# Expert weights in 32 requests of 512 KB, two of them at the beginning, and a reordered start, in an attention and soft-MoE kernel

## The chip, the cores and the metric

The kernel runs on one core of a Trainium2 chip. The metric is the device time of one execution in microseconds (us), as the median of several executions. Beside it there is one execution under the profiler, with a row for each instruction and DMA packet; its times count from the start of its span.

## The reference: what is computed

Attention with 16 extra "beacon" keys and values in front of each head's own, then a soft mixture of experts on its output. Sizes: 8 batches, 8 heads, 576 tokens, head width 64, 16 beacons; 8 experts of 4 slots, width 512, hidden width 1024. All inputs are float32.

```python
k_all = np.concatenate([beacon_k, k], axis=2)      # [8, 8, 592, 64]
v_all = np.concatenate([beacon_v, v], axis=2)
scores = scale * np.matmul(q, k_all.transpose(0, 1, 3, 2))
scores = np.where(causal, -1000000000.0, scores)   # beacons are always seen
a = np.exp(scores - scores.max(-1, keepdims=True))
a /= a.sum(-1, keepdims=True) + 1e-09
attn = np.matmul(a, v_all)                          # -> x [4608, 512]
logits = x @ phi                                    # [4608, 32]
d = softmax over the 4608 tokens;  slot_input = d.T @ x
slot_out[e] = np.maximum(slot_input[e] @ w1[e], 0.0) @ w2[e]
c = softmax over the 32 slots;     out = c @ slot_out      # [4608, 512]
```

The weights w1 [8, 512, 1024] and w2 [8, 1024, 512] are 33.5 MB in float32; q, k and v are 28.3 MB, the output 9.4 MB.

## The kernel before, in words

The work goes by pairs of heads: 4 pairs a batch, 32 pairs in all, numbered n = 4b + g. The order of the instructions on each engine is the order of the calls in the source (a manual schedule), so a waiting instruction holds up everything behind it on its engine. Waits come from the tiles: a tile is free for its next writer when its last reader is done.

For a pair, `scores(n, bank)` (L469) runs the score products of one of four banks on PE, an exponential on ACT (L480) that writes `expT`, and a causal mask on POOL (`affine_select`, L488). `attend(n, hh)` (L493) multiplies by v, the "order products" of the change's name (L502); `normalize(n)` (L506) divides on DVE. `transposes(m, which)` (L445) turns a staged k or q (for two pairs, m = n // 2) on PE, copies it out on DVE (L465), and for k has POOL put two small blocks of beacon keys in front (L455). `cast_v(b, c)` (L378) casts a batch's v to fp16 on POOL in three steps (L384 twice, L388 for the remaining 80 tokens, tile `vrem`), and `perm_v(b)` (L390) reorders it with products on PE. Iteration n of the main loop (L641) holds the scores of pair n, the order products of pair n - 1, and, some pairs later, the transposes of x, `logits`, `dispatch` and `combine_T` of the mixture of experts.

Inputs come by requests of SP, in the order of the calls: `load_qk` (L343; k then q, 576 KB each for half a batch; for the very first half each is cut in two), `load_v` (L352; v, 1 MB, and `vrem`, 160 KB), `load_bv` (L374; beacon_v, 32 KB, into four partitions of the v tile, so that it waits for v to land). They are asked for two batches ahead, as tiles come free (k and q four tiles each, v two). SP's and ACT's requests share eight semaphores in turn, so a request also waits for the landing of the eighth before it. `bkf` (the beacon keys) and `phif` are asked for by ACT.

The weights are cast to fp16 as they are loaded, by requests of POOL: `load_weights(count)` (L430) takes the next `count` of the list `wchunks` (L408), 64 pieces of 256 KB (fp16). Five experts have tiles of their own; the last three go into the tiles of the last batches' k, q and v when those are free (`weight`, L414). Pair n asks for 2 if g = 0, else 1, and from n = 24 on for 2 or 3; what is left is asked for behind the loop (L689). POOL's requests too use eight semaphores in turn.

Behind the loop come the last transposes, logits and dispatch, the experts' first products (`first`, L715), the row sums for the last softmax (`row_sums`, L581, 9 products each), `turn`, the second products (`second`, L732, into `rsps`), and the output: 36 products with the scaling on ACT and DVE, 9.4 MB written by SP. `fill(count, by)` (L573) issues products whose result nobody reads; they stand where PE would have nothing to do.

## Time and profile before

| | us |
|---|---|
| median of 3 runs | 216.74 (215.91 to 219.17) |
| the profiled execution | 219.05 |
| its span, first to last instruction | 217.3 |
| PE busy | 167.5 (77%) |
| DVE, ACT, POOL busy | 134.4, 131.8, 129.4 |
| mean granted clock of PE | 0.90 |
| first order products (L502) | at 25.75 |
| last order products end | at 160.9 |
| second expert products (L736) | 174.2 to 186.3 |
| first product of the output (L797) | at 187.5 |

The profile page has busy time by engine, the span in 40 slices, the DMA queues, the chain of work that ended last, and the costliest groups of instructions. A group's row gives the engine, the operation, the tile written and the tiles read, how often, the busy time, and the idle time before it with what ended that. The slices before, busy tenths of PE, the granted clock, the DMA engines' share and what they moved:

```profile
PE   6932888889899899897897989989878972895400
PEclk9996599999999999999997999999999996587555
DMA  6999999999999999999999975799999999099992
GB/s 177 286 260 323 359 299 316 312 280 300 317 286 283 344 267 280 328 277 280 307 281 274 288 149 93 129 149 178 161 179 175 199 210 189 29 403 412 410 403 98
```

A slice is 5.4 us. GB/s counts what was written: a weight byte in fp16 stands for two read.

### The profile page before, as it was taken

What the parts mean: (1) busy time and instruction counts of PE and PEld (TensorE: products, weight loads), DVE (VectorE), ACT (ScalarE), POOL (GpSimd) and SP (SyncE); (2) the same over time, 40 slices, a digit from 0 to 9 for tenths busy, and PEclk for the clock granted to TensorE, in tenths of its full rate; (3) what the DMA queues carried; (4) which work ended last, traced back from release to release, by engine and by line L of the source; (5) the groups of instructions that cost most, each with busy time, mean ns of one, the idle gap of its engine ahead of it and who ended that gap; (6) DMA issues with size and microseconds to landing.
All of it is one profiled execution on the core that took longest, in us unless ns stands there. A gap on an engine that the chain in (4) does not pass through costs nothing.

```text
span 217.3 us, 7306 instructions
## 1 busy us (share of the span) xinstructions
PE 167.5 (77%) x3080; PEld 109.2 (50%) x3080; DVE 134.4 (62%) x274; ACT 131.8 (61%) x168; POOL 129.4 (60%) x291
## 2 busy tenths in 40 slices
PE   6932888889899899897897989989878972895400
PEld 1511454666666567466584756756755630241100
DVE  0452567787887888885895688888364110498500
ACT  2032587988897899787885889978911310394300
POOL 6027359788688579579576667997885310670000
PEclk9996599999999999999997999999999996587555
DMA  6999999999999999999999975799999999099992
GB/s 177 286 260 323 359 299 316 312 280 300 317 286 283 344 267 280 328 277 280 307 281 274 288 149 93 129 149 178 161 179 175 199 210 189 29 403 412 410 403 98
DMA packets 34309, 55.90 MB, mean 257 GB/s; under 512 B 7740, under 2 KB 16156, under 8 KB 34268
## 3 DMA queue, kind: packets, MB, share of 16 engines
q1 hardware_dynamic: 24444, 38.24, 53.6%
q0 software_dynamic: 9216, 16.78, 43.4%
q8 instruction: 26, 0.43, 0.7%
q10 hardware_dynamic: 608, 0.33, 0.6%
q14 instruction: 15, 0.12, 0.2%
HBM read 62.69 MB, written 9.44 MB: 332 GB/s over the span
## 4 chain that ended last, share of the span: by engine, by line
PE 53%; DMA 23%; ACT 8%; POOL 4%; issue 3%; DVE 2%; ACTq 0%; SPq 0%; POOLq 0%; DVEq 0%
PE av L502 14%; PE sc L475 13%; DMA wt<-in_moe_w_dram 10%; PE trps L463 8%; DMA vstag<-in_v_dram 6%; PE fps L797 5%; PE xtps L527 5%; DMA vstag<-in_beacon_v_dram 4%; ACT expT L480 4%; ACT vh L401 3%; DMA phif<-in_moe_phi_dram 3%; PE vpt L398 2%; PE sips L552 2%; PE lgps L539 2%; PE vps L398 1%
## 5 line engine op out<-in xcount | busy, mean ns | idle before, releaser
L480 ACT ACTIVATE expT<-sc 128x992 f16<-128x992 f32 (+3 forms) x128 | 104.4, 867 | 29.0 <-PE sc L475 27.9
L488 POOL TENSOR_SCALAR_AFFINE_SELECT expT<-expT 128x224 f16<-128x224 f16 (+3 forms) x128 | 55.2, 444 | 40.9 <-ACT expT L480 40.1
L475 PE MATMUL sc<-qT,kT 64*128 64x80 bf16 (+4 forms) x576 | 43.5, 248 | 11.6 <-ACT expT L480 6.0
L502 PE MATMUL av<-vh,expT 128*128 128x65 f16 (+1 forms) x960 | 41.9, 196 | 3.6 <-DVE x L516 1.6
L502 PEld LDWEIGHTS <-expT 128*128 128x128 f16 (+1 forms) x960 | 34.6, 99 | 7.8 <-POOL expT L488 2.7
L475 PEld LDWEIGHTS <-kT 64*128 64x128 bf16 x576 | 17.0, 95 | 27.9 <-issue 22.5
L465 DVE COPY qT<-trps 128x640 bf16<-128x640 bf16 (+1 forms) x32 | 23.3, 770 | 11.3 <-PE trps L463 11.3
L465 DVE COPY kT<-trps 128x640 bf16<-128x640 bf16 (+1 forms) x32 | 23.3, 771 | 10.3 <-PE trps L463 10.3
L516 DVE TENSOR_TENSOR x<-av,r 128x640 f16<-128x640 f32 x32 | 26.4, 825 | 1.2
L800 ACT ACTIVATE osb<-fps,rc 128x512 f32<-128x512 f32 x18 | 11.5, 690 | 17.1 <-PE fps L797 16.8
L384 POOL CAST vc<-vstag 128x512 f16<-128x512 f32 x32 | 18.7, 614 | 1.4 <-DMA vstag<-in_beacon_v_dram 1.4
L531 DVE COPY xT<-xtps 128x576 f16<-128x576 f16 x32 | 14.6, 458 | 6.9 <-PE xtps L527 6.9
L463 PE MATMUL trps<-idb,kstag 128*64 128x128 bf16 x288 | 12.3, 233 | 3.2 <-DMA kstag<-in_k_dram 3.1
L803 DVE TENSOR_SCALAR osb<-fps,rc 128x512 f32<-128x512 f32 x18 | 12.8, 747 | 2.3 <-PE fps L797 1.8
L527 PE MATMUL xtps<-idh,x 128*128 128x128 f16 (+2 forms) x160 | 13.8, 218 | 0.0
L797 PE MATMUL fps<-so,eT 128*128 128x512 f16 x36 | 12.9, 508 | 1.0 <-DVE so L757 0.8
L404 DVE CAST vh<-vpt 128x512 f16<-128x512 f32 x16 | 10.3, 685 | 5.4 <-PE vpt L398 5.4
L398 PE MATMUL vps<-vc,sel 32*128 32x512 f16 x64 | 10.2, 409 | 4.1 <-POOL vc L384 4.1
L401 ACT ACTIVATE vh<-vps 128x1024 f16<-128x1024 f32 x8 | 8.2, 1027 | 7.5 <-PE vpt L398 7.5
L463 PEld LDWEIGHTS <-kstag 128*64 128x64 bf16 x288 | 9.4, 117 | 6.4 <-DMA kstag<-in_k_dram 3.3
L463 PE MATMUL trps<-idb,qstag 128*64 128x128 bf16 x288 | 12.2, 232 | 0.0
L398 PE MATMUL vpt<-vc,sel 32*128 32x512 f16 x64 | 11.4, 407 | 0.3 <-issue 0.3
(87 smaller groups left out, 199.6 us busy)
## 6 DMA issues: line engine op xcount, KB each, us to landing
kstag<-in_k_dram SPq DMA_DIRECT2D x15, 576.0 KB, 14.3
qstag<-in_q_dram SPq DMA_DIRECT2D x15, 576.0 KB, 13.8
out_dram<-osb SPq DMA_DIRECT2D x11, 768.0 KB, 6.7
vstag<-in_v_dram SPq DMA_DIRECT2D x7, 1024.0 KB, 12.2
w1h<-in_moe_w_dram POOLq DMA_DIRECT2D x20, 256.0 KB, 7.3
w2h<-in_moe_w_dram POOLq DMA_DIRECT2D x20, 256.0 KB, 7.1
wt<-in_moe_w_dram POOLq DMA_DIRECT2D x16, 256.0 KB, 8.6
wv<-in_moe_w_dram POOLq DMA_DIRECT2D x8, 256.0 KB, 7.8
```

What stands on the lines that cost most here:

```text
L384: nc.gpsimd.tensor_copy(out=st["c", b][:, :, hs, :].rearrange("p t h d -> p h t d"), in_=st["v", b][:, hs, :, :])
L398: nc.tensor.matmul(outs[c], sel[32 * c:32 * c + 32, t, :], vc[32 * c:32 * c + 32, t, :, :].rearrange("p h d -> p (h d)"), start=(t == 0), ...
L401: nc.scalar.activation(vhs[b % 2][:, 0:2, :, 0:D], ps[:, :, :].rearrange("p c (h d) -> p c h d", d=D), AF.Copy)
L463: nc.tensor.transpose(tp[64 * hh:64 * hh + 64, j - j0, :], t[:, hh, j, :].bitcast(BF)[:, 1::2], idb[:, :])
L465: nc.vector.tensor_copy(out=dst.rearrange("p u (s j) -> p u s j", j=NJ)[:, :, :, j0:j1], in_=tp[:, :, :].rearrange("p j (u s) -> p u s j", ...
L475: nc.tensor.matmul(sc[:, hh, col:col + qw], kTs[n // 2 % 2][po:po + D, n % 2, c * P:(c + 1) * P], qTs[n // 2][po:po + D, n % 2, q0:q0 + qw ...
L480: nc.scalar.activation(ex[:, :, base:base + w], sc[:, :, 0:w], AF.Exp, scale=scale)
L488: nc.gpsimd.affine_select(out=ap, in_=ap, compare_op=AL.is_ge, fill=0.0, base=cbase, pattern=pat, channel_multiplier=-1)
L502: nc.tensor.matmul(av[:, i, :], exps[n % 2][0:KW[c], hh, o:o + P], vhs[b % 2][0:KW[c], c, h, :], start=(c == 0), stop=(c == i))
L516: nc.vector.tensor_tensor(out=xs[b][:, :, head(g, 0):head(g, 1) + 1:2, :].rearrange("p i h d -> p h i d"), in0=av[:, :, :, 0:D], in1=r[:, ...
L527: nc.tensor.transpose(tp[:, QLO[i]:QLO[i] + QW[i]], xs[b][0:QW[i], i, 2 * t:2 * t + 2, :].rearrange("p h d -> p (h d)"), idh[0:QW[i], 0:QW ...
L797: nc.tensor.matmul(fp_[:, :], row_tokens(bb, j), so1[:, :], start=True, stop=True)
```

## The change

1. Weights: 32 requests of 512 KB instead of 64 of 256 KB. A piece of w1 has two rows of 2 KB (fp16) per partition, a piece of w2 one of 4 KB. Two requests are made ahead of everything else that POOL does after its memsets, one behind pair 0's masks; then pairs 2 and 3 one each, up to pair 23 none at g = 0 and one otherwise, from pair 24 on (2, 2, 1)[n % 3]. By pair 23 that is 20 requests (40 old ones, against 30), and by pair 30 all.
2. The start: k's two halves on SP and q's two on ACT, first of all; bkf behind q on ACT; vrem's load apart from v's and later (`load_vr`: batch 0's behind its last q, the others' just ahead of the second half's k); phif on SP behind batch 1's first k and q.
3. k's first transposes ahead of the beacon keys' transposes; half of the first copies of kT and qT on ACT; pair 0's scores, pair 1's first two banks ahead of `perm_v(0)` and of pair 0's order products. Pair 0's masks on POOL come behind the three casts of v. Pairs 0 and 1 are written out; the loop begins at n = 2.
4. More unused products at the start (42 instead of 16 ahead of pair 1's order products), in the `ps_av` banks instead of the scores' banks; fewer behind the loop (9 instead of 15), where three of the four row sums stand in their place.

The diff, cut to its core:

```diff
-            for hh in ((0, 1),) if not first else ((0,), (1,)):
-                lo, hi = 256 * hb + P * hh[0], 256 * hb + P * hh[-1] + P
-                nc.sync.dma_start(
-                    out=t[:, hh[0]:hh[-1] + 1, :, :].rearrange("p h j d -> p h (j d)"),
-                    in_=sr[lo:hi, :].rearrange("(h p) e -> p h e", p=P))
+            eng = nc.scalar if first and tag == "q" else nc.sync
+            for h0, h1 in ((0, 1), (1, 2)) if first else ((0, 2),):
+                lo = 256 * hb + P * h0
+                eng.dma_start(
+                    out=t[:, h0:h1, :, :].rearrange("p h j d -> p h (j d)"),
+                    in_=sr[lo:lo + P * (h1 - h0), :].rearrange("(h p) e -> p h e", p=P))
...
-        nc.sync.dma_start(out=r[0:80, :, :], in_=v[b, :, 496:576, :].rearrange("h p d -> p h d"))
+
+    def load_vr(b):
+        nc.sync.dma_start(out=st["r", b][0:80, :, :],
+                          in_=v[b, :, 496:576, :].rearrange("h p d -> p h d"))
...
     wchunks = [(e, m, j) for es_ in ((0, 1, 2, 3), (4,)) for m in range(2)
-               for e in es_ for j in range(4)]
-    wchunks += [(e, 0, j) for e in (5, 6, 7) for j in range(4)]
-    wchunks += [(e, 1, j) for j2 in range(2) for e in (5, 6, 7) for j in (2 * j2, 2 * j2 + 1)]
+               for e in es_ for j in range(2)]
+    wchunks += [(e, 0, j) for e in (5, 6, 7) for j in range(2)]
+    wchunks += [(e, 1, j) for j in range(2) for e in (5, 6, 7)]
...
         for _ in range(count):
@@ -433,14 +443,24 @@
                 return
             e, m, j = wchunks.pop(0)
             if m == 0:
-                nc.gpsimd.dma_start(out=weight(e, m, j), in_=moe_w1[e, j * P:(j + 1) * P, :])
+                nc.gpsimd.dma_start(
+                    out=piece(e, m, j).rearrange("p (t f) -> p t f", t=2),
+                    in_=moe_w1[e, 2 * j * P:2 * (j + 1) * P, :].rearrange("(t p) f -> p t f", p=P))
             else:
                 src = moe_w2[e].rearrange("(p c) d -> p c d", c=NFC)
                 nc.gpsimd.dma_start(
-                    out=weight(e, m, j),
-                    in_=src[:, 2 * j:2 * j + 2, :].rearrange("p c d -> p (c d)"))
+                    out=piece(e, m, j),
+                    in_=src[:, 4 * j:4 * j + 4, :].rearrange("p c d -> p (c d)"))
...
+            do = dst.rearrange("p u (s j) -> p u s j", j=NJ)[:, :, :, j0:j1]
+            ti = tp[:, :, :].rearrange("p j (u s) -> p u s j", u=2)
+            if m == 0 and j0:
+                nc.scalar.activation(do, ti, AF.Copy)
+            else:
+                nc.vector.tensor_copy(out=do, in_=ti)
...
+        if masked:
+            select(n, bank)
...
-        ps = ps_sc.tile([P, 2, 512], FP, name="fill", tag="sc")
+        pool, tag = (ps_av, "av") if by else (ps_sc, "sc")
+        ps = pool.tile([P, 2, 512], FP, name="fill", tag=tag)
...
     with tc.manual_schedule(engines={ET.PE, ET.DVE, ET.Activation, ET.Pool, ET.SP}):
+        load_qk(0, 0, first=True)
         bkf = work.tile([P, Nb, D], FP, name="bkf", tag="x")
         nc.scalar.dma_start(out=bkf[0:B * H, :, :].rearrange("p n d -> p (n d)"),
                             in_=beacon_k.rearrange("b h n d -> (b h) (n d)"))
-        load_qk(0, 0, first=True)
-        phif = work.tile([P, NDC, NSL], FP, name="phif", tag="phif", bufs=1)
-        nc.scalar.dma_start(out=phif[:, :, :], in_=moe_phi.rearrange("(c p) e -> p c e", p=P))
         load_v(0)
         load_bv(0)
         load_qk(0, 1)
+        load_vr(0)
         load_v(1)
         load_qk(1, 0)
+        phif = work.tile([P, NDC, NSL], FP, name="phif", tag="phif", bufs=1)
+        nc.sync.dma_start(out=phif[:, :, :], in_=moe_phi.rearrange("(c p) e -> p c e", p=P))
+        load_vr(1)
         load_qk(1, 1)
         load_bv(1)
...
-
-
-        fill(8, onesh)
+        load_weights(2)
+
+
+        fill(10, onesh)
+        transposes(0, 0)
+        fill(3, onesh)
...
-        transposes(0, 0)
-        fill(4, onesh)
+        beacon_keys(0)
+        fill(2, onesh)
         transposes(0, 1)
-        fill(4, onesh)
+        fill(6, onesh)
...
-        for n in range(NPAIR + 1):
+
+        scores(0, 0, False)
+        scores(0, 1, False)
+        for c in range(3):
+            cast_v(0, c)
+        fill(3, onesh)
+        scores(0, 2, False)
+        fill(3, onesh)
+        scores(0, 3, False)
+        for bank in range(4):
+            select(0, bank)
+        load_weights(1)
+        fill(3, onesh)
+        scores(1, 0)
+        fill(3, onesh)
+        scores(1, 1)
+        fill(3, onesh)
+        perm_v(0)
+        fill(6, onesh)
+        transposes(1, 0)
+        attend(0, 0)
+        scores(1, 2)
+        transposes(1, 1)
+        attend(0, 1)
+        normalize(0)
+        scores(1, 3)
+        cast_v(1, 0)
+        load_v(2)
+        load_qk(2, 0)
+
+        for n in range(2, NPAIR + 1):
...
+                if b + 2 < B:
+                    if g == 0:
+                        load_v(b + 2)
+                        load_qk(b + 2, 0)
+                    if g == 2:
+                        load_vr(b + 2)
+                        load_qk(b + 2, 1)
+                        load_bv(b + 2)
                 if n == 2:
                     nc.vector.tensor_copy(out=phih[:, :, :], in_=phif[:, :, :])
-                load_weights(2 + n % 2 if n >= 24 else 2 if g == 0 else 1)
+                load_weights((0, 1, 1, 1)[g] if b < 6 else (2, 2, 1)[n % 3])
...
         fill(4)
         x_transposes(NPAIR - 2)
         x_transposes(NPAIR - 1)
+        row_sums(0)
+        logits(B - 1)
+        row_sums(1)
         fill(2)
-        logits(B - 1)
-        fill(4)
         dispatch(B - 1)
         combine_T(B - 1)
...
-        fill(5)
+        row_sums(2)
+        fill(3)
...
         first(0, 0)
         first(0, 1)
-        for bb in range(4):
-            row_sums(bb)
+        row_sums(3)
```

`piece(e, m, j)` gives the tile's part for request j of an expert's w1 or w2, `weight(e, m, c)` now the part of it that one product reads; `beacon_keys(m)` and `select(n, bank)` are the lines taken out of `transposes` and `scores`. `scores(n, bank, False)` leaves the mask to a later `select`.

## The prediction

> **What bounds the kernel now.** The median of the runs shown is 216.74 us; the execution in the profile took 219.05 us, 2.31 more, of which 217.3 is its span. I read four views. First the chain that ended last, at its two ends (start, length in us, what):
>
> ```profile
> 7.93 13.49 DMA vstag<-in_v_dram
> 21.50 9.06 DMA vstag<-in_beacon_v_dram
> 30.76 1.17 POOL vc L384 x2
> ...
> 34.49 0.51 PE av L502 x10
> ...
> 164.55 11.10 DMA wt<-in_moe_w_dram
> ...
> 175.94 9.74 DMA wt<-in_moe_w_dram
> 185.72 1.03 PE rsps L736 x4
> ```
>
> Up to 30.8 us the end hangs on batch 1's v and beacon_v; from 34 to 159 on PE and ACT in turn (the score, exponential and order-product rows between); from 164.55 to 185.72 on the last expert weights. Then the timeline around those two waits (start, length, engine, instruction; in brackets the idle time before it and what ended it):
>
> ```profile
> 30.76 1.17 POOL L384 CAST vc<-vstag 128x512 f16<-128x512 f32 x2 [1.36 <-DMA vstag<-in_beacon_v_dram]
> 33.80 0.92 POOL L488 TENSOR_SCALAR_AFFINE_SELECT expT<-expT 128x512 f16<-128x512 f16 x2
> ...
> 169.47 2.32 PE L585 MATMUL rsps<-ones,eT 128*128 128x1 f16 x36
> 174.21 1.90 PE L736 MATMUL rsps<-w2h,hT 128*32 128x512 f16 x32
> 177.53 0.39 PE L736 MATMUL rsps<-w2h,hT 128*32 128x512 f16 x1 [0.78 <-DVE hT L730]
> ```
>
> POOL waited 1.36 us for beacon_v; pair 2's order products on PE followed at 34.49, after POOL's masks. At 177.53 the second half of the last expert product starts; the first half, the same 32 products, took 1.90. Third, busy time by stage (after the five engines: granted PE clock, DMA share, GB/s):
>
> ```profile
> 9.50:25.00 15.50, 7.46 (x90) 3.52 (x90) 5.88 (x22) 5.17 (x7) 6.21 (x13) 0.76 1.11 308
> 60.00:70.00 10.00, 9.04 (x211) 6.87 (x206) 8.00 (x15) 8.92 (x12) 8.63 (x20) 1.00 1.11 283
> 130.00:135.00 5.00, 4.49 (x110) 3.29 (x104) 4.47 (x10) 4.21 (x6) 3.65 (x8) 1.00 0.46 65
> 175.00:180.00 5.00, 3.38 (x50) 1.33 (x39) 0.69 (x1) 0.03 (x1) 0.89 (x2) 1.00 1.12 210
> ```
>
> [...] So the DMA is full at the beginning, with inputs alone; full in the loop; and half empty at 130 to 135, where the inputs have run out and weights come only as POOL asks. Fourth, the queues of one stage, 165 to 180 us (packets, MB written, share of 16 engines):
>
> ```profile
> q0 software_dynamic: 1639, 2.98, 109.1%
> ```
>
> Only weights run there: 2.98 MB is 11.4 requests of 256 KB in 15 us, **1.32 us each on a full DMA**. That is my price for weight traffic.
>
> **The change, part by part.**
>
> *The end.* The schedule now has all 32 requests asked for by pair 30; before, 14 of 64 were left after pair 31. From pair 24 on 12 requests (24 old ones) are to come; at 1.32 that is 32 us, and the seven pairs from 24 to 30 last about that (4.3 us each: 34 to 159 us for 29 pairs), so the last lands some 5 us after it is asked for, and the second half of L736, some 20 us behind, finds it there. Without waits it ends at 177.53 + 1.90 = 179.43; it ended at 185.72 + 0.61 = 186.33. **Gain 6.9.** Late next is PE's own chain (normalising, transposes, logits, dispatch, first products), not a DMA.
>
> *Row sums.* 27 of the 36 products of L585 move from between the first products into places where unused products stood while PE waited for ACT or DVE; the ones they replace take about as long (row_sums(1) and fill(2) for fill(4) ahead of the dispatch). 27/36 of 2.32: **gain 1.7**. If they were hidden already, 0; but first(1,0) at 171.72 came straight behind them with no wait shown, so I take all.
>
> *Two requests at the beginning, a third after pair 0's masks.* By the time batch 1's beacon_v lands, the DMA then carries 6 old requests of weights where it carried 2 (issued at 21.59). The window from 9.5 to 25 shows 1.11 with inputs alone, so nothing hides the rest: 4 x 1.32 = **5.3 us later for beacon_v**, at 35.8. The low bound is 2.6, if the third request (POOL stands at the cast of vrem before it, whose load is now behind k and q) is served after beacon_v; the high bound is 5.9, by the whole run's mean (q0's 43.4% of 217.3 us over 64). I take 5.3. Queued behind that cast on POOL are pair 2's four masks, and on PE pair 2's order products. POOL then has 1.17 + 0.81 + 0.52 + 0.92 = 3.4 us of work where 3.7 passed before (the request between moves away), and pair 3's first exponentials (1.83) are already done. Catch-up lies between 0.3 and 2.1; I take 1.3, nearer the middle. **Loss 4.0.**
>
> *Scores ahead, q on ACT, beacon keys later, POOL's masks after the casts, phi later.* All of it moves work inside the first 28 us. Pair 0's order products started at 25.75 and may come some us sooner or, because the masks now stand behind the cast that needs vrem, not at all sooner. Both end in front of the wait for beacon_v, which ends last, so I count 0. If beacon_v did not bind, this could be worth as much as PE's idle stretch before the first v products, up to 4 us. The q request on ACT's queue moves ahead of bkf: SP is freed of 2 issues (0.90 us), and SP's next requests wait for landings anyway: 0. On ACT half of the first two copies is added (0.7 us each, the DVE row's halves) while DVE does the other half: 0. phi's cast is at pair 2, after all of it: 0.
>
> *More unused products.* From 16 to 42 ahead of pair 1's order products (0.43 us each at half clock, 0.2 at full): at most 26 x 0.43 = 11 us of PE, in a stretch where PE was busy 7.46 of 15.5 us and waits for ACT and DMA: 0, cover being the same wait for beacon_v. Above it, they cost a us; below, they save the half clock (next).
>
> *PE's clock.* PE will stand idle for some us ahead of pair 2's order products. In the profile PE idles for 3.1 and for 4.1 us between 13 and 21, and the clock from 20 to 30 is 0.61; from 115 to 120 it is 0.66, and a pair takes about 1 us longer there than its neighbours. So a wait of 5 us can bring one or two pairs at a lower clock: 0 to 2 us. PE's waiting for ACT may absorb it, as at the first place; I take 0 in the sum, and 2 is a rival below.
>
> *32 requests of 512 KB.* POOL issued each in 0.55 us, and POOL is on the chain for 4%. Half as many save between 0 (if a request of two rows per partition takes twice as long) and 32 x 0.55 x 4%, under 1 us: 0.
>
> *Six old requests a batch instead of five, batches 1 to 5.* One more is 1.32 us a batch, 6.6 in all. Against it: the share can rise from about 1.09 (90 to 100 us) to 1.12, some 2.3 us over the loop, and beacon_v had slack. It was asked for at 65.73 for batch 4; q ahead of it, asked for at 63.58, lands 13.8 later (median) at 77.4; the cast was at 80.53: 3.1 us. So 6.6 - 2.3 - 3.1 = 1.2 is left at most and 0 if the DMA shares better; **loss 0.5**.
>
> **Sum:** -6.9 - 1.7 + 4.0 + 0.5 = -4.1: the profiled execution from 219.05 to 214.95, the median from 216.74 to **212.6**.
>
> **Rivals.**
>
> *The loop starves (slower).* Inputs wait for the larger weight packets in every batch, with no slack and no better share: 5.3 + 6.6 + 2 for the clock + 1 for the unused products, 14.9 lost against 8.6 gained: 216.74 + 6.3 = 223. For it: share 1.11 before anything is added. Against: POOL waited for beacon_v once, and never for another v. It turns slower than before where the loop ends more than 8.6 us later.
>
> *Weights for less (faster).* The early weights run beside inputs at little loss, because the first 25 us moved 308 GB/s while k and q alone ran at 380 to 400 within it; or the start gains what its reordering suggests. Then the loss is 0 and up to 4 are won: 216.74 - 8.6 = 208, at best 204. Against: 1.11. The Trainium skill, "DMA: Bandwidth & Descriptors", section "Bandwidth", has the rule that DMAs be batched to 1 MiB or more, with a fixed cost of about 2 us each in "Anatomy of one DMA"; requests were landing every 1.32 us with several under way, so no run here shows that cost on the path.
>
> *PE at a lower clock behind the wait.* The 2 us above come on top: 214.6. For it: the 0.61 behind two idle stretches shorter than the one I expect. Against: pair 3's scores, queued ahead of the wait, keep PE in work for part of it. The Trainium skill, "TensorE: Matmul & The Clock Gate", section "Part 1: The HAM clock gate", states that after a window of about 3.4 us without work the array runs at half rate; by that rule this rival is the outcome, and the trace agrees at the 0.61.
>
> *The weights are still late.* Slots for the last experts come free only as the last batches' k, q and v are used, and POOL asks in order. If a request stands for a slot, the end keeps half its wait: 3.4 back, 216.0. Against: each slot's last reader is at least one pair ahead of the request in the program.
>
> **Chances.** Forecast 0.38, weights for less 0.25, starving loop 0.14, still late 0.12, lower clock 0.11. The forecast's own range: startup loss 1 to 6 and loop 0 to 1.2 instead of 4.5 together, and up to 1.7 less for the row sums, give 209 to 217. The range of 8 in 10 reaches to 207 and 220. Two per cent, about what a measurement can tell from no change, is 4.3 us: faster means under 212.4. That takes all of "weights for less" and half of the forecast: faster 0.44; slower (over 221.1) 0.09, from the starving loop; within 0.47.
>
> **What would show it.** Right: no PE wait on a weight DMA in the second expert products, which follow the last pair some 8.6 us sooner than before (25.4 us lay between 160.9 and 186.3); 9 row sums between the first products instead of 36; a POOL wait of some us on beacon_v at the second v cast, ending near 36; DMA share still 1.1 at the beginning, and no 0.46 at 130. Wrong: beacon_v landing by 31 (the price of early weights), pair 2's order products before 34.5, or POOL waits for v in later batches. The forecast falls most easily with the 5.3.

## The result, and the profile after

The changed kernel takes 225.61 us, the median of four runs (225.09 to 227.62). The kernel before, run beside it, took 217.73 (215.91 to 219.17). The ratio is 1.041, 95% interval 1.029 to 1.053: slower. The forecast was 212.6, with a range of 207 to 220; the nearest rival was the starving loop, 223. The profiled executions compare as 227.62 us after and 219.05 before, with spans of 225.8 and 217.3, so 8.5 us more of span are to be explained. The runs of some kernels below fall into two groups some per cent apart; a ratio is always of the faster group, and where it could not be formed the range of the runs stands with the time of the profiled one. A place in the loop is read from one profiled execution; the five kernels here that ask for the bytes of 30 old requests by pair 23, and for none early, end their loops within 1.6 us of each other (159.8 to 161.4).

Begin at the end, where the gain was forecast. These are rows of PE's timeline after the change (start, length, engine, line, tiles; idle time and what ended it in brackets):

```profile
186.56 0.70 PE L610 MATMUL rsps<-ones,eT 128*128 128x1 f16 x9
...
189.69 1.90 PE L792 MATMUL rsps<-w2h,hT 128*32 128x512 f16 x32
...
193.01 0.39 PE L792 MATMUL rsps<-w2h,hT 128*32 128x512 f16 x1 [0.78 <-DVE hT L786]
```

One group of nine row sums is left between the products, and the second half of the last expert products (193.01) waits for DVE and no longer for weights. The last rows of these products, first before the change and then after it, are:

```profile
185.73 1.00 PE L736 MATMUL rsps<-wt,hT 128*32 128x512 f16 x2
...
194.54 0.38 PE L792 MATMUL rsps<-wt,hT 128*32 128x512 f16 x2
```

Before, they end at 186.73 (the 186.3 in the table ahead is the end of a row beside this one), 25.8 us behind the last order product at 160.93. After, they end at 194.92, 16.8 us behind the last order product at 178.09: **9.0 won**, near the forecast 8.6.

So the loop lost 17.2 us, not 4.5 (17.2 less 9.0 is 8.2; the output behind takes 0.3 longer). The starts of the order products of some pairs, read from the trace, tell where:

| pair | before | after | difference |
|---|---|---|---|
| 0 | 25.7 | 25.1 | -0.6 |
| 2 | 33.5 | 37.4 | +3.9 |
| 3 | 39.4 | 45.8 | +6.4 |
| 9 | 63.8 | 70.8 | +7.0 |
| 19 | 108.7 | 118.4 | +9.7 |
| 23 | 128.2 | 136.1 | +7.9 |
| 26 | 139.5 | 152.0 | +12.5 |
| 27 | 145.1 | 161.6 | +16.5 |
| 28 | 148.9 | 166.0 | +17.1 |
| 31 | 159.6 | 176.8 | +17.2 |

There are two big steps, one at pairs 2 and 3 and one between pairs 23 and 28. POOL's rows at the two places:

```profile
35.84 1.17 POOL L388 CAST vc<-vstag 128x512 f16<-128x512 f32 x2 [6.99 <-issue]
...
149.04 1.17 POOL L388 CAST vc<-vstag 128x512 f16<-128x512 f32 x2 [5.91 <-DMA vstag<-in_beacon_v_dram]
```

The second is the cast of v waiting for beacon_v. For the first the profile names nothing that ended the wait ("issue"). That it was beacon_v too is inferred from runs below: the cast came at 29.74 with no early requests, and pair 2's order products at 32.8 instead of 37.4 where that beacon_v is not loaded. Its time, 35.84, is as forecast (35.8). It does not stay the only wait, as POOL's waits show (waiter, what for: us in all, times, longest):

```profile
POOL vc L388 <- DMA vstag<-in_beacon_v_dram: 13.2, 5, 5.9
POOL vc L388 <- issue: 7.0, 1, 7.0
```

Before, there was one such wait, of 1.36 us. The chain that ended last says what has become of the loop:

```profile
57.84 15.68 DMA vstag<-in_v_dram
73.54 15.67 DMA vstag<-in_beacon_v_dram
89.33 1.17 POOL vc L388 x2
...
95.30 15.72 DMA vstag<-in_v_dram
111.08 15.85 DMA vstag<-in_beacon_v_dram
126.98 1.17 POOL vc L388 x2
```

The forecast's kernel had PE and ACT in this stretch. Here it is a ring of transfers. Batch by batch, v takes 15.7 us to land; beacon_v, which waits for that and then stands behind k and q in SP's queue, takes as long again; POOL casts; the tile is free; the next v is asked for. Whether the ring is the cause or only the path is asked below. Last, busy time by stage after the change (five engines, granted PE clock, DMA share, GB/s):

```profile
30.00:40.00 10.00, 4.27 (x73) 2.60 (x70) 3.57 (x8) 3.59 (x5) 4.04 (x10) 0.85 1.08 325
...
60.00:70.00 10.00, 8.15 (x181) 5.71 (x174) 8.29 (x16) 7.82 (x11) 5.27 (x13) 1.00 1.10 250
...
130.00:140.00 10.00, 8.60 (x188) 6.03 (x188) 7.79 (x17) 7.57 (x10) 8.14 (x20) 1.00 1.09 252
...
150.00:160.00 10.00, 6.69 (x72) 4.01 (x74) 3.12 (x7) 2.64 (x4) 8.88 (x19) 0.50 0.90 158
```

The DMA is as full at 130 to 140 (1.09) as in the whole loop; it was at 0.46 between 130 and 135 before. The last beacon_v is still on its way: SP asked for it at 130.13, and it was cast at 149.04. And behind the wait at 149 PE runs from 150 to 160 at half clock (0.50).

What is open: whether the loss comes from the requests at the beginning, from six old requests a batch instead of five, from the size of a request, from the bulk behind pair 24, or from beacon_v's place in the queue.

### The profile page after: what moved, and what is told of

Read it like the earlier page. It is cut to its first block, busy times and chain, and to the rows that moved or that the text cites. A ratio compares the mean times of both kernels' runs of the same rounds, so it can differ in the third digit from the quotient of the medians.

```text
span 225.8 us, 7315 instructions
## 1 busy us (share of the span) xinstructions
PE 173.1 (77%) x3100; PEld 112.9 (50%) x3100; DVE 132.8 (59%) x272; ACT 133.3 (59%) x170; POOL 115.1 (51%) x259
## 4 chain that ended last, share of the span: by engine, by line
DMA 35%; PE 32%; POOL 10%; ACT 6%; issue 6%; DVE 4%; ACTq 0%; DVEq 0%; POOLq 0%; SPq 0%
DMA vstag<-in_beacon_v_dram 14%; DMA vstag<-in_v_dram 14%; PE av L526 6%; PE sc L506 5%; POOL expT L497 4%; PE fill L602 4%; DMA bkf<-in_beacon_k_dram 4%; ACT expT L511 4%; POOL vc L388 4%; DMA out_dram<-osb 3%; PE trps L480 3%; PE xtps L551 2%; PE vps L402 2%; PE hps L777 2%; PE rsps L792 2%
## 5 line engine op out<-in xcount | busy, mean ns | idle before, releaser
L497 POOL TENSOR_SCALAR_AFFINE_SELECT expT<-expT 128x224 f16<-128x224 f16 (+3 forms) x128 | 54.5, 439 | 33.3 <-ACT expT L511 32.4
L526 PE MATMUL av<-vh,expT 128*128 128x65 f16 (+1 forms) x960 | 44.5, 199 | 16.4 <-POOL expT L497 13.1
L506 PE MATMUL sc<-qT,kT 64*128 64x80 bf16 (+4 forms) x576 | 44.6, 252 | 10.2 <-ACT expT L511 5.3
L526 PEld LDWEIGHTS <-expT 128*128 128x128 f16 (+1 forms) x960 | 36.2, 101 | 21.5 <-POOL expT L497 17.6
L487 DVE COPY kT<-trps 128x640 bf16<-128x640 bf16 (+1 forms) x31 | 22.7, 772 | 15.2 <-PE trps L480 15.2
L487 DVE COPY qT<-trps 128x640 bf16<-128x640 bf16 (+1 forms) x31 | 22.6, 771 | 8.1 <-PE trps L480 7.6
L540 DVE TENSOR_TENSOR x<-av,r 128x640 f16<-128x640 f32 x32 | 26.4, 824 | 1.1
L602 PE MATMUL fill<-eT,onesh 128*128 128x512 f16 x42 | 14.6, 488 | 1.5 <-POOL onesh L631 1.5
L408 DVE CAST vh<-vpt 128x512 f16<-128x512 f32 x16 | 10.3, 685 | 8.3 <-PE vpt L402 8.3
L858 DVE TENSOR_SCALAR osb<-fps,rc 128x512 f32<-128x512 f32 x18 | 12.1, 742 | 1.9 <-PE fps L852 1.0
L551 PEld LDWEIGHTS <-x 128*128 128x128 f16 (+2 forms) x160 | 9.5, 102 | 5.5 <-issue 5.1
L852 PE MATMUL fps<-so,eT 128*128 128x512 f16 x36 | 10.4, 405 | 1.2 <-DVE so L812 0.8
```

What stands on the lines that cost most here:

```text
L487: nc.vector.tensor_copy(out=do, in_=ti)
L497: nc.gpsimd.affine_select(out=ap, in_=ap, compare_op=AL.is_ge, fill=0.0, base=cbase, pattern=pat, channel_multiplier=-1)
L506: nc.tensor.matmul(sc[:, hh, col:col + qw], kTs[n // 2 % 2][po:po + D, n % 2, c * P:(c + 1) * P], qTs[n // 2][po:po + D, n % 2, q0:q0 + qw ...
L526: nc.tensor.matmul(av[:, i, :], exps[n % 2][0:KW[c], hh, o:o + P], vhs[b % 2][0:KW[c], c, h, :], start=(c == 0), stop=(c == i))
L540: nc.vector.tensor_tensor(out=xs[b][:, :, head(g, 0):head(g, 1) + 1:2, :].rearrange("p i h d -> p h i d"), in0=av[:, :, :, 0:D], in1=r[:, ...
L551: nc.tensor.transpose(tp[:, QLO[i]:QLO[i] + QW[i]], xs[b][0:QW[i], i, 2 * t:2 * t + 2, :].rearrange("p h d -> p (h d)"), idh[0:QW[i], 0:QW ...
```

## The experiments

In all of them "loop's end" is the end of the last order product: 160.9 before, 178.1 after the change.

### Which half of the change, and is it the early requests or the packets?

**Without the early requests.** The three are asked for by pairs 2, 3 and 4 instead, one more each.

```diff
-        load_weights(2)
...
-        load_weights(1)
...
-                load_weights((0, 1, 1, 1)[g] if b < 6 else (2, 2, 1)[n % 3])
+                load_weights((0, 1, 1, 1)[g] + (n < 5) if b < 6 else (2, 2, 1)[n % 3])
```

> The changed kernel without the three early weight requests; they are asked for by pairs 2, 3 and 4 instead, one more each. Theory (weights in flight hold up the inputs, beacon_v last): batch 1's beacon_v is cast near 30.5 us instead of 35.8, pair 3's order products start near 40 instead of 45.8, and the time falls by 4 to 6, to 220 to 222; what is lost at pairs 26 to 28 stays. Rival (the new order of the start costs the time: masks behind the cast that needs vrem, vrem and phi late): pair 3 stays near 45 and the time at 225.

Measured: median 227.03 (222.71 to 227.94, profiled 226.80), loop's end 177.7. Both expectations missed: pair 3 came at 37.8, and the time did not fall. Up to pair 9 the pairs ran 1.3 to 1.8 us ahead of the kernel before (pair 9 at 62.5 against 63.8), so the start's reordering is worth that where no weights are asked for ahead of pair 2. Then POOL stood 10.2 us for beacon_v, and pair 10 came 6.7 us later than before. The delay is not bound to the beginning: the same three requests, made by pairs 2 to 4, were followed by a wait of this size for the next batch's beacon_v.

**w2 in rows of 2 KB.** The requests stay at 512 KB; w2's rows in them are halved.

```diff
-            return w2h[e][:, 4 * j:4 * j + 4, :].rearrange("p c d -> p (c d)")
+            return w2h[e].rearrange("p (a b i) d -> p a b (i d)", a=2, b=2)[:, :, j, :]
...
-                    in_=src[:, 4 * j:4 * j + 4, :].rearrange("p c d -> p (c d)"))
+                    in_=src.rearrange("p (a b i) d -> p a b (i d)", a=2, b=2)[:, :, j, :])
```

> The changed kernel with each request for w2 in two rows of 2 KB a partition instead of one of 4 KB; same requests, same bytes, same order. If a queue's turn in a DMA engine is one packet, the weights' share beside inputs falls from about 75% and POOL's waits for beacon_v at 89 and 108 us (2.1 and 3.0) fall under 1.5 each: 221 to 224. If only bytes count: no difference beyond 1 us, 225 to 226.5.

Measured: median 225.15, but runs from 218.49 to 227.99 (profiled 223.55); loop's end 174.1. The two waits for beacon_v that were to fall under 1.5 us were 1.85 each. By its time the run is inconclusive; the size of a request is taken up further down.

**The start alone**: the new order, the row sums and the unused products, with the weights in 256 KB requests as before.

```diff
-               for e in es_ for j in range(2)]
+               for e in es_ for j in range(4)]
...
-        load_weights(2)
...
-                load_weights((0, 1, 1, 1)[g] if b < 6 else (2, 2, 1)[n % 3])
+                load_weights(2 + n % 2 if n >= 24 else 2 if g == 0 else 1)
...
```

> The changed kernel's start, order of requests and row sums, with the weights as before: 64 requests of 256 KB on the old schedule. Theory: beacon_v is cast near 30.5, no POOL wait for v in later batches, the wait for the last weights comes back; 214 to 218. Rival (the order of the start costs the time): 221 or more, with pair 3's order products behind 42.

Measured: 220.10 us, ratio 1.017 (1.007 to 1.028), loop's end 161.4, no POOL wait for beacon_v. The loop ends with that of the kernel before (160.9); the second expert products wait 6.4 us for weights and end 26.4 us behind it (25.8 before). The row sums win nothing as long as that wait ends last. The 1.7% in time is more than was expected, and it was not taken apart.

**The weights alone**: the kernel before with the changed requests of 512 KB and their schedule (the lines that build the requests are left out here).

```diff
...
+        load_weights(2)
...
-                load_weights(2 + n % 2 if n >= 24 else 2 if g == 0 else 1)
+                load_weights((n == 0) if n < 2 else (0, 1, 1, 1)[g] if b < 6 else (2, 2, 1)[n % 3])
```

> The kernel before with the changed weight requests and their schedule alone (two at the beginning, one behind pair 0's masks), all else as before, row sums too. Theory: the whole loss is here, with POOL waits for beacon_v as in the changed kernel; 225 to 229. Rival: the weights alone win what was forecast for the end, 209 to 214.

Measured: 228.18 us, ratio 1.057 (1.047 to 1.066), loop's end 175.1, POOL waits for beacon_v of 14.0 us in five places. So the weights' requests alone bring the loss: 14.2 of the 17.2 us at the loop's end, and the time of the changed kernel and more, since the row sums stand as before.

### Is it beacon_v's place in the queue?

**beacon_v right behind v**, so that it neither waits for v nor stands behind k and q; for that, v leaves the beacon rows alone and comes in two requests.

```diff
-        if b:
-            lo = (b * H * S - Nb) * D
+        for p0, p1 in ((4, 116), (116, 128)):
...
                         load_v(b + 2)
+                        load_bv(b + 2)
...
-                        load_bv(b + 2)
```

> The changed kernel, with v loaded for every batch in two requests that leave the four beacon partitions alone, and beacon_v asked for right behind them, so that it neither waits for v to land nor stands behind k and q of the second half. Theory (the loop's loss of 17.2 us is the casts of v waiting for beacon_v, each wait holding the next batch's requests back): the POOL waits for beacon_v, 13.2 us in five places after the change, fall under 3 us in all, the last order products end by 168 instead of 178.1, and the time is 208 to 215. Rival (the DMA's bytes bound whatever the order): k and q land later by what beacon_v gains, PE waits for transposes instead, and the time stays at 220 or more.

Measured: 236.44 us, ratio 1.085 (1.075 to 1.094), loop's end 187.6. The time is far from what the theory said. POOL's waits for beacon_v did shrink to 6.0 us, but PE now waited for k:

```profile
PE trps L473 <- DMA kstag<-in_k_dram: 18.7, 8, 4.6
```

**The same two edits in the kernel before**, as a control.

> The kernel before with the same two edits to v and beacon_v. Theory: the kernel before waits for beacon_v only once, 1.36 us at the second cast, so that is all there is to win; the end still waits 6.9 us for weights: 214 to 217 beside a before of 216 to 218. Rival (the longer requests of k and q lose as much): no change or up to 2 us slower.

Measured: 225.75 us, ratio 1.043 (1.035 to 1.051), loop's end 168.1. So the two edits cost some 7 us with the old weights too, and the run above is no clean test of beacon_v. SP's timeline in this kernel tells why (the time is that of SP's issuing):

```profile
58.79 9.10 SPq L361 DMA_DIRECT2D vstag<-in_v_dram  x2
67.98 0.64 SPq L365 DMA_DIRECT2D vrem<-in_v_dram  x1
68.68 3.58 SPq L368 DMA_DIRECT2D vstag<-in_beacon_v_dram  x1
72.35 0.39 SPq L348 DMA_DIRECT2D kstag<-in_k_dram  x1
```

From the first row of v to the request of k 13.6 us pass, and k is what PE then waits for (9.5 us in five waits; 3.1 in one before).

**No beacon_v at all** for batches 1 to 7, with v's single request kept: the clean form of the question. The four beacon rows of v are left out of the computation.

```diff
     def load_bv(b):
+        if b:
+            return
```

> The changed kernel without the loads of beacon_v for batches 1 to 7 (left out of the computation: the four beacon rows of v hold other rows of v there), seven requests of 32 KB. Nothing else differs, so no request of SP is longer or in another place. Theory (v, then beacon_v behind k and q, is a latency loop that carries the loss): the five POOL waits, 13.2 us, go or become a wait for v of under 3 us, the last order products end by 168 instead of 178, and the time is 212 to 217. Rival (the inputs' own share of the DMA is what fails): k, q or v is late by as much, PE waits for transposes or POOL for v, and the time stays over 221.

Measured: median 219.84 (214.66 to 221.79, profiled 219.70), loop's end 170.0. POOL's waits for beacon_v are gone, and 8.1 of the 17.2 us with them. But all of that is won by pair 3 (37.8 against 45.8), at the first wait. From pair 3 to pair 23 the loop takes 90.2 us without beacon_v and 90.3 with it, and from there to its end 42.0 in both. In place of v and beacon_v, the chain that ended last now runs through the transfers of k (five of them from 27.7 to 117.3 us), and PE waits for k:

```profile
PE trps L482 <- DMA kstag<-in_k_dram: 9.7, 6, 5.6
```

So the rival holds behind the first wait, though its number missed: whichever input comes last, it comes late, and as late. The ring with beacon_v is the path of a lateness that has another source.

### How much do the weights cost the loop, and does the request's size matter?

**All weights behind the loop.** Only the loop is of interest here.

```diff
-        load_weights(2)
...
-        load_weights(1)
...
-                load_weights((0, 1, 1, 1)[g] if b < 6 else (2, 2, 1)[n % 3])
```

> The changed kernel with all 32 weight requests behind the loop, so that the loop runs on inputs alone; the end is then some 60 us longer and its time says nothing. What counts is the end of the last order products: 160.9 before, 178.1 after the change. If PE and ACT carry the loop and inputs alone never wait: at 29 pairs of 3.75 us from some 30 us, 140 to 148, with no POOL wait for beacon_v. If the loop is slow for another reason than weights (the order of the start, the clock): 155 or more.

Measured: loop's end 156.5 (time 272.42). With inputs alone the DMA has room to spare, as two of its stages show:

```profile
60.00:70.00 10.00, 8.43 (x196) 6.22 (x194) 7.30 (x16) 7.90 (x12) 6.90 (x16) 1.00 0.30 100
...
120.00:130.00 10.00, 8.88 (x191) 6.01 (x189) 8.79 (x19) 8.58 (x11) 5.20 (x14) 1.00 0.02 3
```

The expected 140 to 148 was too low by its start and its pace (pair 3 to 23 in 84.6 us, 4.2 a pair). What follows, by single profiles: before the change the weights cost the loop 4.4 us (160.9 against 156.5), after it 21.6.

**Size alone**: the kernel before with 512 KB requests at the old bytes by pair, two or three a batch, none early.

```diff
...
-                load_weights(2 + n % 2 if n >= 24 else 2 if g == 0 else 1)
+                old = [2 + i % 2 if i >= 24 else 2 if i % 4 == 0 else 1 for i in range(n + 1)]
+                load_weights(sum(old) // 2 - sum(old[:n]) // 2)
```

> The kernel before with requests of 512 KB at the same bytes by the same pair as before (two or three a batch instead of five), none early and seven of them left behind the loop. Theory (packets of 2 and 4 KB in larger requests take the DMA from the inputs' 1 KB packets): the loop ends 5 to 10 us later than before and POOL waits for beacon_v over 5 us; the end still waits for weights: 221 to 227. Rival (more bytes earlier is what costs, size is nothing): the last order products end within 2 us of before's 160.9 and the time is 215 to 219.

Measured: 218.92 us, ratio 1.011 (1.006 to 1.015), loop's end 160.5, no POOL wait for beacon_v. The theory that larger requests take the DMA from the inputs is out at these bytes: the loop ends as before. The queues agree. From 40 to 115 us, with 512 KB requests (q1 inputs, q0 weights; packets, MB written, share):

```profile
q1 hardware_dynamic: 13182, 16.15, 68.5%
q0 software_dynamic: 2386, 5.58, 38.8%
```

and before, with 256 KB, in the same stretch:

```profile
q1 hardware_dynamic: 12978, 16.05, 67.4%
q0 software_dynamic: 3170, 5.77, 40.9%
```

### Is it the bulk behind pair 24?

**Fewer requests ahead of the last beacon_v**, in the changed kernel.

```diff
-                load_weights((0, 1, 1, 1)[g] if b < 6 else (2, 2, 1)[n % 3])
+                load_weights((0, 1, 1, 1)[g] if b < 6 else 1 + (n > 25))
```

> The changed kernel, with one weight request each at pairs 24 and 25 and two each at pairs 26 to 30, instead of 2, 2, 1 in turn: three requests fewer ahead of the last beacon_v. Theory: the last POOL wait for beacon_v, 5.91 us at 149.0, and the half clock behind it (some 3 us) go for the most part; earlier batches stay as they are, so 217 to 221, with the last order products ending at 170 to 174 and still no wait for weights in the second expert products. Rival (the last batch is late because all before it was, and its beacon_v waits for v whatever the weights do): 224 to 227.

Measured: 223.96 us, ratio 1.031 (1.023 to 1.040), loop's end 174.9; the last part won 3.2 us of 17.2, and POOL still waited 12.0 us for beacon_v. The edit does less than was said of it: ahead of the cast that waits for the last beacon_v, pair 24 asks for one request (at 139.38) instead of two (from 139.23), so one is missing there and not three. The cast's last wait was 4.80 us instead of 5.91, and PE's behind it 2.65 instead of 4.47. The rival's time is nearer, and 174.9 of 178.1 stay; but with one request moved this is a weak test of the bulk.

**The bulk of 256 KB requests alone**, in the kernel before.

```diff
-                load_weights(2 + n % 2 if n >= 24 else 2 if g == 0 else 1)
+                load_weights((2, 4, 6, 6, 6, 5, 5, 0)[n - 24] if n >= 24 else 2 if g == 0 else 1)
```

> The kernel before with only its requests of 256 KB from pair 24 on changed: 2, 4, 6, 6, 6, 5, 5, so that all are asked for by pair 30 and none is left behind the loop. Theory: the end's wait for weights, 6.9 us, is won at little loss, since the last beacon_v is on its way before the bulk: 210 to 213. Rival (any bulk of weights ahead of the last casts holds beacon_v of batch 7 up, as after the change): POOL waits over 3 us at the last cast of v, and 215 or more.

Measured: 226.90 us, ratio 1.045 (1.035 to 1.054), loop's end 174.1. Both theories missed. No cast waited for beacon_v; it is POOL itself that ran out of time (POOL's timeline):

```profile
146.00 1.10 POOL L436 DMA_DIRECT2D wv<-in_moe_w_dram  x2
147.06 1.09 POOL L436 DMA_DIRECT2D wt<-in_moe_w_dram  x2
148.76 0.53 POOL L436 DMA_DIRECT2D wt<-in_moe_w_dram  x1 [0.61 <-DMA w2h<-in_moe_w_dram]
150.09 0.53 POOL L436 DMA_DIRECT2D wt<-in_moe_w_dram  x1 [0.79 <-DMA w2h<-in_moe_w_dram]
150.62 0.75 POOL L488 TENSOR_SCALAR_AFFINE_SELECT expT<-expT 128x224 f16<-128x224 f16 x2
```

Each request takes about 0.55 us of POOL, and the last two here also waited 0.61 and 0.79 us for an earlier one to land. Six of them stand 4.6 us ahead of the masks (146.00 to 150.62). It goes on so to pair 31: PE's order products waited 10.3 us for masks in all, and from 150 to 170 the granted clock was 0.67 to 0.68.

**The bulk in 512 KB requests**: the kernel before up to pair 23, then 2 small and 1 large and 2, 2, 3, 3, 3, 2 large ones.

```diff
...
-                load_weights(2 + n % 2 if n >= 24 else 2 if g == 0 else 1)
+                load_weights((3, 2, 2, 3, 3, 3, 2, 0)[n - 24] if n >= 24 else 2 if g == 0 else 1)
```

> The kernel before, 256 KB requests as before up to pair 23 and then 512 KB: 2 small and 1 large at pair 24, then 2, 2, 3, 3, 3, 2 large ones, so that all are asked for by pair 30 with 17 requests of POOL instead of 34. Theory (what cost the bulk of 256 KB requests was POOL's own time and its waits for the eighth request before, ahead of the masks): the last order products end by 164, the second expert products wait for no weights, and the time is 210 to 214. Rival (bytes ahead of the last inputs and masks cost whatever their number): last order products at 170 or later and 217 or more.

Measured: median 213.06 (210.22 to 215.02, profiled 212.45) beside 217.18 for the kernel before, span 210.7, loop's end 159.8, as the theory had it. The second expert products wait for no weights and end at 179.8, where the prediction put them for a kernel without that wait (179.43). So the bulk behind pair 24 costs nothing where the loop is not already late and POOL makes few requests of it.

### Early requests against rate

What is left is a square of two parts. The three runs below and the changed kernel all have its start and its row sums. "Early" is the pair of requests ahead of everything; the rate up to pair 23 is three requests of 512 KB a batch (six old ones) or two and a half (five).

**Early, old rate.**

```diff
-                load_weights((0, 1, 1, 1)[g] if b < 6 else (2, 2, 1)[n % 3])
+                old = [2 if i % 4 == 0 else 1 for i in range(n + 1)]
+                load_weights(sum(old) // 2 - sum(old[:n]) // 2 if n < 24 else (2, 2, 2, 2, 2, 3, 2, 0)[n - 24])
```

> The changed kernel with the requests at the beginning kept, then two and a half a batch as before the change (17 by pair 23 instead of 20), and 15 from pair 24 to 30. If the rate is the cause: the late beacon_v at 36 costs 4 to 6 us up to pair 3 as after the change, nothing is added in the loop behind it, the last order products end at 162 to 168, time 210 to 216. If the early requests are the cause (a batch late once stays in a loop of v, beacon_v and cast): they end at 173 or later and the time is 219 or more.

**New rate, not early.**

```diff
-        load_weights(2)
...
-                load_weights((0, 1, 1, 1)[g] if b < 6 else (2, 2, 1)[n % 3])
+                load_weights((0, 1, 1, 1)[g] if b < 6 else 2)
```

> The changed kernel without the two requests ahead of everything, with three a batch as after the change (18 by pair 23) and two each from pair 24 to 30. If the rate is the cause: no loss up to pair 9, then POOL waits for beacon_v of 3 us and more, and the last order products end at 170 or later, time 218 or more (as where the early requests were asked for by pairs 2 to 4). If the early requests are the cause: order products end by 165, time 209 to 214.

**Neither.**

```diff
-        load_weights(2)
...
-                load_weights((0, 1, 1, 1)[g] if b < 6 else (2, 2, 1)[n % 3])
+                old = [2 if i % 4 == 0 else 1 for i in range(n + 1)]
+                load_weights(sum(old) // 2 - sum(old[:n]) // 2 if n < 24 else (2, 2, 2, 3, 3, 3, 2, 0)[n - 24])
```

> The changed kernel with neither: one request behind pair 0's masks, then two and a half a batch (15 by pair 23), and 17 from pair 24 to 30. Both theories: no loss in the loop, last order products by 160, 17 us from there to the end of the second expert products as after the change (16.9), the rest as there (31): a span of 207 to 210 and a time of 209 to 212, under both kernels. If it is over 215, the new start itself costs the loop something that the weights hid.

| | time, us | loop's end | pair 3 | pair 23 | asked for by pair 23 |
|---|---|---|---|---|---|
| early, new rate (the change) | 225.61 (225.09 to 227.62) | 178.1 | 45.8 | 136.1 | 20 |
| new rate, not early | 222.84 (216.02 to 223.72) | 174.3 | 39.7 | 132.2 | 18 |
| early, old rate | 212.99 (212.21 to 213.71) | 164.4 | 45.9 | 131.7 | 17 |
| neither | 211.58 (211.19 to 217.37) | 161.4 | 39.8 | 126.3 | 15 |

With the early requests the rate costs the loop's end 13.7 us (178.1 - 164.4) and the time 12.6, far beyond the spread of either kernel's runs. Without them the profiles give 12.9 (174.3 - 161.4), but there the profile is of the longest of four runs, 223.72, and the shortest, 216.02, lies only 4.4 above the median of "neither". So without the early requests the size of the rate's cost stays open, from 4 to 13 us. With the old rate the early requests cost 3.0 at the loop's end (164.4 - 161.4) and 1.4 in time. Against the kernel before, "early, old rate" has a ratio of 0.988 (0.980 to 0.997) and "neither" 0.983 (0.976 to 0.991); the latter has the lowest median of all that ran, span 209.7. POOL's waits for beacon_v tell the same. Early with the old rate, it is the one place that was forecast and a remainder:

```profile
POOL vc L388 <- issue: 6.9, 1, 6.9
...
POOL vc L388 <- DMA vstag<-in_beacon_v_dram: 1.8, 1, 1.8
```

and with the new rate, though the pair ahead of everything is missing, in that longest run:

```profile
POOL vc L388 <- DMA vstag<-in_beacon_v_dram: 16.6, 5, 7.5
```

**How a sixth request becomes 13 us.** By pair 23 three requests of 512 KB more have been made than with the old rate. That is six old ones, one in pairs 2 and 3 and one in each of batches 1 to 5, and 7.9 us at 1.32. The loop is later there by 4.4 us with the early requests (136.1 - 131.7), and by 5.9 without in the profiles (132.2 - 126.3). The remaining 9.3 of the 13.7 come behind pair 23, and the two traces with the early requests split them. From pair 23 to pair 26 it takes 15.9 us against 11.4 with the old rate. The 4.5 more are one wait of PE for the masks behind the cast at 149.04:

```profile
152.04 0.70 PE L526 MATMUL av<-vh,expT 128*128 128x65 f16 x5 [4.47 <-POOL expT L497]
```

From pair 26 to pair 28 it takes 14.0 us against 9.2 with the old rate. In that stretch PE shows no other wait over 0.82 us; the granted clock is 0.50 up to 162 and 0.83 from there, where the old rate has 1.00 at the same pairs. From pair 28 on both take 12.1 us. So a late input and the half clock behind it cost about as much each; the clock was not changed by itself.

Why that input was late is seen in part. SP's requests for the last v and its beacon_v, after the change:

```profile
114.11 0.37 SPq L363 DMA_DIRECT2D vstag<-in_v_dram  x1
...
130.13 1.99 SPq L379 DMA_DIRECT2D vstag<-in_beacon_v_dram  x1
```

and early with the old rate:

```profile
108.99 0.37 SPq L363 DMA_DIRECT2D vstag<-in_v_dram  x1
...
120.03 2.72 SPq L379 DMA_DIRECT2D vstag<-in_beacon_v_dram  x1
```

v is asked for 5.1 us later and takes 16.0 us to land instead of 11.0, so beacon_v is asked for 10.1 later, and its cast came at 149.04 instead of 138.73, 10.3 later. Why 32 KB of beacon_v then took 18.9 us up to its cast, with most of the DMA on weights (q0 90.3% of the packets' time from 135 to 145, q1 15.2%), was not taken apart. Without beacon_v a wait of 5.6 us for k stands in the same place (at 152.0), so the ring is not needed for it.

## Why the prediction was wrong, step by step

- **Six old requests a batch instead of five**, put at 0.5, is the step that failed: with the early requests it cost 13.7 us at the loop's end and 12.6 in time. Up to pair 23 its price and its slack fit: with the old request more that pairs 2 and 3 make as well, the gross price is 7.9; less the slack of 3.1 it is 4.8, and 4.4 to 5.9 were measured. The credit of 2.3 for a rising share was not there: the share was about 1.09 before, and the changed kernel's stages from 40 to 140 us show 1.06 to 1.10. What the step had no term for is the end of the loop, 9.3 us: it priced batches 1 to 5 and took nothing for the last inputs, which now came late, one wait of 4.5 us with 4.8 at half clock behind it.
- **Two requests at the beginning**, put at 4.0: beacon_v's cast came at 35.84 against 35.8 forecast, so the price of early weights was right. The catch-up of 1.3 did not come, and the clock, put at 0, added: from pair 2 to pair 3 it takes 8.4 us with early requests and 6.4 without, at 0.85 and 0.81 in the changed kernel's stages from 30 to 50 us. Pair 3 was 6.1 us late by that ("early, old rate" against "neither"). Half of it was made up later, and 3.0 are left at the loop's end. That this is near 4.0 is partly luck: two errors of the step offset each other.
- **The end** and **row sums**, together 8.6: 9.0. Right. The difference is in the reading of the old end, 186.33, where the last of these products ended at 186.73. The run of the start alone agrees that the row sums count only once the weights are no longer late.
- **Scores ahead**, 0: the start is worth 1.3 to 1.8 us up to pair 9 where no weights are asked for ahead of pair 2, but with one request there pair 3 comes as before (39.8 against 39.4), and the loop's end does too (161.4 against 160.9). Right where it counts.
- **32 requests of 512 KB**, 0: in the loop the size is worth nothing (160.5 against 160.9). In the bulk of the last pairs it is worth much (159.8 with large requests, 174.1 with small ones): the bound of under 1 us had averaged POOL's issues over the whole run.
- **PE's clock**, 0 with a rival of 2 us: about 2.0 behind the first wait, as the rival had it, and 4.8 behind the last, which no term of the forecast had. By the rule that the prediction cites from the Trainium skill's "TensorE: Matmul & The Clock Gate", section "Part 1: The HAM clock gate", the array runs at half rate after a window of about 3.4 us without work. The trace agrees: PE's order products stood 4.47 us for a mask of POOL ahead of the stage at 0.50.
- **More unused products**, 0: not tried by itself.
- **The rivals.** The starving loop, given 0.14, is nearest: its 223 against 225.61, and POOL did wait for beacon_v in later batches. Its reason, larger packets of weights, is not it: at the same bytes the larger requests cost the loop nothing. Its 14.9 is near the 17.2 partly by luck, since the early requests cost less than its 5.3 and the last pairs much more than its 2 for the clock. "The weights are still late" did not happen: the second expert products waited for no weights. "PE at a lower clock" was right at the first wait. With the old rate the forecast's own terms hold: 212.99 (0.988 of the kernel before) against the 212.1 that the sum gives without the rate's 0.5.

## What to carry to other kernels

Where the DMA is full over a whole loop, traffic added in every round is paid in every round, less the slack that can be used up once; and a share that reads full did not read fuller here. Price the end of the loop too: there one late input cost 4.5 us, and PE's lower clock behind it as much again. A ring of waits in the trace may be only the path of a delay: taking beacon_v out of it left the pace as it was, with k in its place. Move such traffic to where the inputs have run out, and in few requests, since the engine that issues them has its own work.

## What the runs showed of the hardware

- A full DMA and a DMA that is too full look alike: 1.09 at 130 us in the loop that lost, and 1.09 from 70 to 100 us in the loop before. Here the time at which the share falls (before at 120, after at 140) and the waits tell them apart. The share is the packets' time over 16 engines' time, and it is over 1 even where one queue runs almost alone (q0 109.1% from 165 to 180 before).
- Behind PE's wait of 4.47 us up to 152.04 the granted clock was 0.50 to 162, and two pairs took 14.0 us instead of 9.2.
- Two queues shared the DMA nearly the same with weight requests of twice the size (q0 38.8% against 40.9% of the packets' time at 5.58 and 5.77 MB).
- SP's issue of a request lasted from 0.27 us (beacon_v at 55.23) to 8.88 (k at 58.26) after the change. In the control, v in two requests, the second of 12 partitions, held SP for 9.10 us. The Trainium skill's "DMA: Bandwidth & Descriptors", section "Why a DMA increments its semaphore by 16 and not by 1", states that a request uses the largest number of engines, up to 16, that divides the outermost dimension of both sides; by that, 12 partitions go to 12 of the 16 engines and 128 to all. No run here separates that from the mere wait behind the first request.
- A POOL request of 512 KB in two rows per partition took 0.71 to 0.73 us of POOL, one in a single row 0.55, as much as one of 256 KB before.
